# A cached-attention decode step with a gated MLP: the output weights in four transfers instead of five, six filler products instead of three, and two bias rows loaded by another engine

## The chip, the cores and the metric

The kernel runs on one core of a Trainium2 chip. Five engines share the work: TensorE (PE in the profile, its weight loads PEld) multiplies, VectorE (DVE) does the elementwise work and the reductions, ScalarE (ACT) copies and computes exponentials, GpSimd (POOL) only sets a few constants here, and SyncE (SP) issues transfers. Sixteen DMA engines bring data from the chip's memory. An engine works through its instructions in order and waits on semaphores. The metric is the device time of one execution in microseconds (us).

## The reference: what is computed

Two tokens (B = 2, one position each, D = 512) pass a layer normalisation; the result feeds two branches:

```python
xn = _layernorm(x)
s = attention(xn @ wq, k_cache, v_cache) @ wo     # 32 heads of 128, 8192 cached positions
h = gelu(_layernorm(xn) @ w1 + b1)                # 512 -> 1376
g = silu(h @ w2 + b2)                             # 1376 -> 512
out = x + s * g
```

Everything is float32. The caches hold 2 x 32 x 8192 x 128 numbers each, 268 MB for the keys and as much for the values. wq and wo have 8.4 MB each, w1 and w2 2.8 MB each; b1 has 5.4 KB and b2 2 KB.

## The kernel before

**The stream.** Nearly all transfers go through one queue, SyncE's, written out by hand in program order: w1, w2, wq, the first keys in two halves, then keys and values by turns, each turn (n = 0 to 31) 8.4 MB of keys and 8.4 MB of values, and at the end wo. A transfer is issued when its buffer has been read out, so SyncE waits for engines, not for data. There are two big buffers for keys and one (`vb`) for values. At the start `vb` holds all the small things of the boot stage instead, w1, w2, b1, b2 and the MLP's intermediates; the first values wait until the boot is through with it.

**The boot.** While the first weights arrive, the kernel makes its constants, normalises x, runs the whole MLP down to `gate` (function `mlp`), and forms the queries with wq. In `mlp`, each of three stretches of w1 ends with a product that adds b1 (L412); the four products that add b2 come last (L462). x, b1 and b2 are issued by ScalarE's queue (L337, L339), the rest by SyncE's (function `load`, L314).

**The turns.** VectorE multiplies keys by queries (L524) and sums (L531); TensorE, VectorE and ScalarE turn the sums into exponentials; TensorE multiplies them into the values (`weighted`, L575) and folds the result (L584). The turns 1 to 30 are a loop; the last one is written out behind it, and takes its values from a key buffer, so that `vb` is free for wo one turn earlier.

**The tail.** wo is read as 32 rows of 512 numbers per partition, and arrives in pieces; `WO_PIECES` gives the rows at which they begin and end. SyncE issues all pieces together once L575 of the turn before the last has read `vb` out. TensorE's order behind the last turn's products is: the sums of all heads (L632, L634), then `busy(3)`, then rows 0 to 23 of wo, then the rest. `busy(n)` (L562) issues n products of the identity with the queries, 128x512 each, into a scratch bank that nobody reads. Rows 0 to 23 (`WIDE` is 24) are multiplied as 128x512 products into `wide` (L648), which ScalarE then copies to SBUF (L651); rows 24 to 28 go as four 128x128 products each into `acc` (L657), then four products fold the copy of `wide` in (L662), then rows 29 to 31 follow (L657 again). Each row's product waits for its piece (function `piece`). VectorE multiplies `acc` by `gate` and adds x (L666, L667), and SyncE stores the result (L668).

Each float32 product stands in the trace as two matmul records, so that 24 products of L648 make 48 records.

Of the kernel before, what the change touches and what calls it, by code (L numbers as in the profile page):

```python
# [21 lines left out]
class Plan:  # L22
# [18 lines left out]
    def op(self, eng, fn, r=(), w=(), over=(), it=None, loop=False, dma=None):  # L41


        o = Op()
        o.eng, o.fn, o.it, o.loop, o.dma, o.tell = eng, fn, it, loop, dma, False
        need = {}

        def after(d, war):
            if d.dma is None and dma is None and d.eng == eng and (eng == "pe" or war):
                return  # L50
            if d.dma is None:
                if need.get(d.eng) is None or need[d.eng].idx < d.idx:
                    need[d.eng] = d
            else:
                k = ("dma", d.dma)
                if need.get(k) is None or need[k].idx < d.idx:
                    need[k] = d

        for k in r:
            if k in self.writer:  # L60
                after(self.writer[k], False)
        for k in list(w) + list(over):
            if k in self.writer:
                after(self.writer[k], False)
            for d in self.readers.get(k, ()):
                after(d, True)
        clock = self.clock[eng]
        need = {k: d for k, d in need.items() if clock.get(k, 0) < d.idx}
        o.deps = [(k, d) for k, d in need.items()
                  if not any(e is not d and e.done.get(k, 0) >= d.idx for e in need.values())]  # L70
        for _, d in o.deps:
            for k, v in d.done.items():
                clock[k] = max(clock.get(k, 0), v)
        own = eng if dma is None else ("dma", dma)
        self.count[own] = o.idx = self.count.get(own, 0) + 1
        o.done = dict(clock)
        o.done[own] = o.idx
        for k in w:
            self.writer[k] = o
            self.readers[k] = []  # L80
        for k in r:
            if k not in w:
                self.readers.setdefault(k, []).append(o)
        self.ops.append(o)
# [80 lines left out]
def decode_kernel(nc, x, kc, vc, wq, wo, w1, b1, w2, b2, out):  # L165
# [31 lines left out]
    op = plan.op  # L197

    def pe(fn, r=(), w=(), it=None, loop=False):
        op("pe", fn, r, w, it=it, loop=loop)  # L200

    def dve(fn, r=(), w=(), it=None, loop=False):
        op("dve", fn, r, w, it=it, loop=loop)
# [58 lines left out]
    def take(name, p, n, base=0, at=None):  # L262

        if at is None:
            at = used[0]
            used[0] += n
            assert used[0] <= KP * DH
        boot.append(name)
        return vb[base:base + p, at:at + n]
# [7 lines left out]
    b1_sb = take("b1", 1, F, R, at)  # L277
    b2_sb = take("b2", 1, D, R, at + F)
# [34 lines left out]
    def load(dst, src, sem, w, over=()):  # L313
        op("sp", lambda: nc.sync.dma_start(dst, src), (), w, over=over, dma=sem)  # L314

    def load_k(n):
        i = (n + 1) % 2
        if n in (0, N - 1):
            for s in range(2):
                load(kbuf[i][:, s * M:(s + 1) * M], kf[n][:, s * M:(s + 1) * M], f"k{i}{s}", [("kb", i, s)])  # L320
            return
        load(kbuf[i], kf[n], f"kb{i}", [("kb", i, s) for s in range(2)])


    WO_PIECES = (0, 16, 24, 29, 31, 32)
    WIDE, FOLD = WO_PIECES[-4:-2]


    load(w1_sb, w1.rearrange("(p c) f -> p c f", p=P), "w1", ["w1"])
    load(w2_sb, w2.rearrange("f n -> (f n)").rearrange("(p e) -> p e", p=P), "w2", ["w2"])  # L330
    load(wq_sb, wq.rearrange("(p c) n -> p c n", p=P), "wq", [("kb", 0, s) for s in range(2)])
    load_k(0)

# [1 line left out]
    dve(lambda: nc.vector.memset(eps_t, EPS), w=["eps"])  # L335
    act(lambda: nc.scalar.activation(warm, eps_t, AF.Sqrt), ["eps"], ["warm"])
    op("act", lambda: nc.scalar.dma_start(x_sb, x.rearrange("b s d -> (b s) d")), w=["x"], dma="x")  # L337
    for t, src, k in ((b1_sb, b1, "b1"), (b2_sb, b2, "b2")):
        op("act", lambda t=t, src=src: nc.scalar.dma_start(  # L339
            t.rearrange("o (k e) -> o k e", k=16), src.rearrange("(o k e) -> o k e", o=1, k=16)), w=[k], dma=k)  # L340


    pool(lambda: nc.gpsimd.memset(ident, 0.0), w=["ident"])
# [144 lines left out]
    for k in range(N // NB):  # L488

        b, e = divmod(k, HH // NB)  # L490
# [68 lines left out]
    def busy(n):  # L559

        for _ in range(n):
            pe(lambda: matmul(scratch[3], ident, Q[:, :512], start=True, stop=True),  # L562
               ["ident"] + [("Q", k) for k in range(512 // (NB * DH))], ["s3"])
# [55 lines left out]
    wo_r = wo.rearrange("(p c) n -> p c n", p=P)  # L619
    for i, (a, e) in enumerate(zip(WO_PIECES, WO_PIECES[1:])):  # L620
        load(wo_sb[:, a:e], wo_r[:, a:e], f"wo{i}", [("wo", i)], over=["vb"])
# [8 lines left out]
    for b in range(B):  # L630
# [2 lines left out]
           ["ones"] + [("ZR", n) for n in own], ["OA"])  # L633
        pe(lambda b=b: matmul(OA[:, b, :OC], Z[:, b * P:(b + 1) * P], mod, start=True, stop=True),  # L634
           ["mod"] + [("Z", n) for n in own], ["OA"])
    busy(3)
    dve(lambda: nc.vector.reciprocal(rl, OA[:, :, OC]), ["OA"], ["rl"])
    dve(lambda: nc.vector.tensor_tensor(out=on[:, ::RB], in0=OA[:, :, :OC],
                                        in1=rl.unsqueeze(2).to_broadcast([P, B, OC]), op=ALU.mult),
# [2 lines left out]
    def piece(c):  # L642
        return ("wo", max(i for i, a in enumerate(WO_PIECES[:-1]) if a <= c))

# [52 lines left out]
```

## Time and profile before

| | |
|---|---|
| median of 3 runs | 1300.4 us (1300.06 to 1300.45) |
| profiled execution: its own time | 1300.03 us |
| profiled execution: its span in the trace | 1298.2 us |
| DMA engines: share of the span in SyncE's queue | 99.7% |
| moved | 559.39 MB, 431 GB/s |
| VectorE busy | 1134.6 us, 87% |
| TensorE busy | 404.8 us, 31% |
| wo's five pieces, issue to landing | 19.0, 23.5, 26.1, 26.9, 27.1 us |

The span runs from the first to the last instruction of the traced execution; 1.83 us of its own time lie outside. The DMA engines are full from the first microseconds to the landing of wo's last piece, so the span is the length of the stream plus what lies before its first byte and behind its last. A line of a view of instructions gives its start, its length, the engine, the source line, the operation and the tiles, and in brackets how long the engine had been idle before it and what ended that.

### The profile page before, as it was taken

How to read it: one execution, taken by the hardware profiler on the slowest of the kernel's cores; microseconds unless marked ns; L12 is line 12 of the kernel's file. 1: busy time of each engine (PE TensorE's matmuls, PEld its weight loads, DVE VectorE, ACT ScalarE, POOL GpSimd, SP SyncE). 2: the span in 40 equal slices, each digit the busy share in tenths (PEclk: the TensorE clock that was granted, in tenths of full speed). 3: DMA queues.
4: the chain of work that ended last, by engine and by line, in shares of the span. 5: the costliest groups of instructions: out<-in, count | busy, mean ns of one | idle time of the engine just before them, and what ended most of it. 6: DMA issues, size and time to landing. Idle time of an engine off the chain costs nothing.

```text
span 1298.2 us, 6788 instructions
## 1 busy us (share of the span) xinstructions
PE 404.8 (31%) x2728; PEld 123.9 (10%) x2728; DVE 1134.6 (87%) x276; ACT 77.6 (6%) x250; POOL 1.4 (0%) x8
## 2 busy tenths in 40 slices
PE   5602333312333312333321333321233321233337
PEld 1100011000101000101000101100001000001103
DVE  3599999888889988889988888988888988888991
ACT  1100000000000000000000000000000000000000
POOL 0000000000000000000000000000000000000000
PEclk9856666556666656666656666656666655666658
DMA  9999999999999999999999999999999999999998
GB/s 406 445 423 440 430 432 436 426 444 428 438 430 432 438 426 440 430 434 434 428 442 428 438 430 430 440 426 440 430 434 434 430 438 430 438 430 430 427 433 363
DMA packets 10826, 559.39 MB, mean 431 GB/s; under 512 B 1208, under 2 KB 1216, under 8 KB 1476
## 3 DMA queue, kind: packets, MB, share of 16 engines
q1 hardware_dynamic: 10812, 559.29, 99.7%
q8 instruction: 4, 0.07, 0.0%
q14 instruction: 2, 0.02, 0.0%
q10 hardware_dynamic: 8, 0.01, 0.0%
HBM read 559.30 MB, written 0.00 MB: 431 GB/s over the span
## 4 chain that ended last, share of the span: by engine, by line
DMA 74%; PE 24%; DVE 1%; issue 0%; ACT 0%; SPq 0%; DVEq 0%
DMA vb<-in_A_v_cache_dram 72%; PE po L575 22%; DMA vb<-in_A_wo_dram 2%; PE s L410 1%; PE po L482 1%; PE s L452 0%; PE s L412 0%; PE acc L657 0%; DVE vb L418 0%; ACT L431 0%; DVE vb L356 0%; PE s L459 0%; SPq L314 0%; DVE vb L367 0%; DVE vb L444 0%
## 5 line engine op out<-in xcount | busy, mean ns | idle before, releaser
L524 DVE TENSOR_TENSOR kb<-kb,Q 128x8192 f32<-128x8192 f32 x64 | 555.5, 8681 | 105.2 <-DMA kb<-in_A_k_cache_dram 95.9
L531 DVE TENSOR_REDUCE sc<-kb 128x64 f32<-128x8192 f32 x64 | 552.3, 8665 | 0.0
L575 PE MATMUL po<-vb,PZ 128*8 128x512 f32 x1984 | 280.7, 730 | 292.8 <-DMA vb<-in_A_v_cache_dram 292.8
L547 PE MATMUL s<-nm,srow 1*128 1x2 f32 x64 | 18.7, 359 | 364.0 <-DVE nm L541 364.0
L575 PEld LDWEIGHTS po<-vb,PZ 128*8 128x8 f32 x1984 | 56.4, 103 | 491.0 <-issue 489.5
L538 PE MATMUL s<-ident,mx 128*1 128x128 f32 x32 | 11.8, 369 | 192.7 <-DVE mx L535 192.7
L547 PEld LDWEIGHTS s<-nm,srow 1*128 1x128 f32 x64 | 15.9, 307 | 373.3 <-DVE nm L541 373.3
L582 ACT COPY o<-po 128x512 f32<-128x512 f32 x32 | 18.7, 585 | 533.3 <-PE po L575 533.3
L548 ACT COPY bias<-s 128x2 f32<-128x2 f32 x32 | 5.1, 160 | 622.1 <-PE s L547 622.1
L584 PE MATMUL s<-mod,o 128*128 128x2 f32 x256 | 33.6, 253 | 22.1 <-ACT o L582 22.1
L584 PEld LDWEIGHTS s<-mod,o 128*128 128x128 f32 x256 | 31.0, 191 | 51.3 <-ACT o L582 51.3
L552 ACT ACTIVATE PZ<-sc,bias 64x128 f32<-64x128 f32 x64 | 25.5, 399 | 1.8
L538 PEld LDWEIGHTS s<-ident,mx 128*1 128x1 f32 x32 | 2.5, 79 | 196.2 <-DVE mx L535 165.7
L590 DVE TENSOR_TENSOR Z<-blk,s 128x8 f32 (+1 forms) x32 | 5.2, 163 | 13.3 <-PE s L584 13.3
L418 DVE COPY vb<-vb 2x384 f32<-2x384 f32 x4 | 1.8, 500 | 15.9 <-ACT vb L414 15.9
L410 PE MATMUL s<-vb 128*2 128x512 f32 (+1 forms) x24 | 12.5, 673 | 0.3 <-ACT vb L375 0.3
L552 ACT ACTIVATION_READ_ACCUMULATOR PZ<-sc,bias 64x1 f32 x64 | 11.8, 185 | 0.0
L666 DVE TENSOR_TENSOR gate<-acc,gate 128x128 f32<-128x128 f32 x1 | 0.3, 291 | 12.1 <-PE acc L657 12.1
L535 DVE TENSOR_REDUCE mx<-sc 128x1 f32<-128x128 f32 x32 | 9.2, 286 | 1.1
L556 ACT ACTIVATE ZR<-half,rs 128x8 f32 (+1 forms) x32 | 9.6, 301 | 4.1
L575 PE MATMUL po<-kb,PZ 128*8 128x512 f32 x64 | 9.4, 755 | 1.4 <-ACT PZ L552 1.4
L541 DVE TENSOR_REDUCE nm<-s 1x2 f32<-1x128 f32 x32 | 8.7, 272 | 0.3 <-PE s L538 0.3
(88 smaller groups left out, 84.5 us busy)
## 6 DMA issues: line engine op xcount, KB each, us to landing
kb<-in_A_k_cache_dram SPq DMA_DIRECT2D x4, 4096.0 KB, 43.5
kb<-in_A_v_cache_dram SPq DMA_DIRECT2D x2, 4096.0 KB, 40.9
vb<-in_B_w_dram SPq DMA_DIRECT2D x2, 2752.0 KB, 12.5
vb<-in_A_wo_dram SPq DMA_DIRECT2D x1, 4096.0 KB, 19.0
vb<-in_A_wo_dram SPq DMA_DIRECT2D x1, 2048.0 KB, 23.5
vb<-in_A_wo_dram SPq DMA_DIRECT2D x1, 1280.0 KB, 26.1
vb<-in_A_wo_dram SPq DMA_DIRECT2D x1, 512.0 KB, 26.9
vb<-in_A_v_cache_dram SPq DMA_DIRECT2D x31, 29.5
```

Of the source, the lines that this page charges most:

```text
L410: pe(lambda f=f, w=w, ph=ph, c=c: matmul(ph[:B, :w], yT[:, c, :], w1_sb[:, c, f:f + w], start=(c == 0), stop=False), ["yT", "w1"], [k])
L482: pe(lambda i=i, c=c, wv=wv, a=a, j=j, hd=hd: matmul(PO[R * j:R * j + NQ * B, :].rearrange("m (h d) -> m h d", d=DH), xnT[:, c, a:a + NQ * ...
L524: vector(n, n, lambda n: nc.vector.tensor_tensor(out=k, in0=k, in1=cols(Q, n * DH, DH).unsqueeze(1).to_broadcast([P, M, DH]), op=ALU.mult) ...
L531: vector(n, n, lambda n: nc.vector.tensor_reduce(out=SC[:, s * M:(s + 1) * M], in_=k, axis=AX.X, op=ALU.add), [("kb", i, s)], [("sc", s)])
L535: vector(n, n, lambda n: nc.vector.tensor_reduce(out=MX, in_=SC, axis=AX.X, op=ALU.max), [("sc", 0), ("sc", 1)], ["mx"])
L538: pe(lambda i: transpose(PM[:1, :P], MX, ident), ["mx", "ident"], ["s1"], it=n, loop=n > 0)
L547: pe(lambda i: matmul(PN[:, :U], srow, NM, start=True, stop=True), ["srow", "nm"], ["s2"], **one)
L552: act(lambda i, r=r, s=s: nc.scalar.activation(PZ[r, :, s, :], sc[r], AF.Exp, bias=BIAS[r, s:s + 1], scale=SCALE, accum_out=RS[r]), ["bias ...
L556: act(lambda i: nc.scalar.activation(cols(ZR, i * UP - UP, UP), half, AF.Copy, scale=RS), ["half"] + [("rs", s) for s in range(U)], [("ZR" ...
L575: pe(lambda i, t=t, j=j, v=v: matmul(PO[R * j:R * j + U * JW, :], PZ[:, t].rearrange("p s j -> p (s j)"), v[:, t * JW:(t + 1) * JW, :].rea ...
L582: act(lambda i: nc.scalar.copy(O4, PO), ["po"], ["o4"], **one)
L584: pe(lambda i, k=k: matmul(PT[:, :U], O4[:, k * DH:(k + 1) * DH], mod[:, k:U * JW:JW], start=(k == 0), stop=(k == JW - 1)), ["o4", "mod"], ...
```

## The change

- `WO_PIECES` becomes (0, 24, 29, 31, 32): wo arrives in four transfers, the first of which holds rows 0 to 23. `WIDE` and `FOLD` stay 24 and 29, and the products are the same in the same order.
- `busy(3)` becomes `busy(6)`.
- b1 and b2 are issued by SyncE, between w2 and wq, instead of by ScalarE behind x.

```diff
-    WO_PIECES = (0, 16, 24, 29, 31, 32)
+    WO_PIECES = (0, 24, 29, 31, 32)
     WIDE, FOLD = WO_PIECES[-4:-2]
...
     load(w2_sb, w2.rearrange("f n -> (f n)").rearrange("(p e) -> p e", p=P), "w2", ["w2"])
+    for t, src, k in ((b1_sb, b1, "b1"), (b2_sb, b2, "b2")):
+        load(t.rearrange("o (k e) -> o k e", k=16), src.rearrange("(o k e) -> o k e", o=1, k=16), k, [k])
     load(wq_sb, wq.rearrange("(p c) n -> p c n", p=P), "wq", [("kb", 0, s) for s in range(2)])
...
     op("act", lambda: nc.scalar.dma_start(x_sb, x.rearrange("b s d -> (b s) d")), w=["x"], dma="x")
-    for t, src, k in ((b1_sb, b1, "b1"), (b2_sb, b2, "b2")):
-        op("act", lambda t=t, src=src: nc.scalar.dma_start(
-            t.rearrange("o (k e) -> o k e", k=16), src.rearrange("(o k e) -> o k e", o=1, k=16)), w=[k], dma=k)
...
-    busy(3)
+    busy(6)
     dve(lambda: nc.vector.reciprocal(rl, OA[:, :, OC]), ["OA"], ["rl"])
```

## The prediction

> **What bounds the kernel now.** I read the page first, for the shares: SyncE's queue fills the DMA engines for 99.7% of the span. Then the chain that ended last, in order of time, for the tail:
>
> ```profile
> 1266.71 0.43 SPq L314
> 1267.15 0.06 issue
> 1267.20 26.14 DMA vb<-in_A_wo_dram
> 1293.34 0.04 issue
> 1293.38 1.31 PE acc L657 x34
> 1294.70 0.22 PE acc L662 x7
> 1294.91 0.83 PE acc L657 x23
> 1295.75 0.02 issue
> 1295.77 0.30 DVE gate L666
> ```
>
> The columns are start, length, and what ran. The end hangs on transfers up to 1293.34; behind that only 2.4 us of products, 0.6 us of VectorE and the store remain. Then TensorE's timeline of that stretch:
>
> ```profile
> 1266.99 1.05 PE L584 MATMUL s<-mod,o 128*128 128x2 f32 x8 [0.71 <-ACT o L582]
> ...
> 1283.03 2.82 PE L562 MATMUL s<-Q,ident 128*128 128x512 f32 x6
> 1285.78 3.67 PE L648 MATMUL wide<-vb,on 128*17 128x512 f32 x32
> 1290.30 1.94 PE L648 MATMUL wide<-vb,on 128*17 128x512 f32 x16 [0.85 <-DMA vb<-in_A_wo_dram]
> 1293.38 1.31 PE L657 MATMUL acc<-vb,on 128*17 128x128 f32 x40 [1.15 <-DMA vb<-in_A_wo_dram]
> 1294.50 0.41 PE L662 MATMUL acc<-o,mod 128*17 128x128 f32 x8
> 1294.72 0.99 PE L657 MATMUL acc<-vb,on 128*17 128x128 f32 x24
> ```
>
> TensorE keeps up with wo: rows 0 to 15 (x32) are done at 1289.45, before rows 16 to 23 are there; these (x16) are done at 1292.24, before the third piece is there. Third, the issues of wo on the page, with the time to landing:
>
> ```profile
> vb<-in_A_wo_dram SPq DMA_DIRECT2D x1, 4096.0 KB, 19.0
> vb<-in_A_wo_dram SPq DMA_DIRECT2D x1, 2048.0 KB, 23.5
> vb<-in_A_wo_dram SPq DMA_DIRECT2D x1, 1280.0 KB, 26.1
> vb<-in_A_wo_dram SPq DMA_DIRECT2D x1, 512.0 KB, 26.9
> ```
>
> Added to the issues (1266.34, 1266.71, 1267.20) that makes landings at 1285.3, 1290.2 and 1293.3; the last two pieces follow at about 1294.6 and 1295.2 (26.9 and 27.1 us from issues some 0.4 us apart). Fourth, TensorE's granted clock, in stretches of time (columns: stretch, its length, busy time and instructions of PE, PEld, DVE, ACT, POOL, granted clock, DMA share, GB/s). I come back to these:
>
> ```profile
> 1187.09:1190.50 3.41, 2.25 (x20) 1.07 (x12) 3.41 (x1) 0.58 (x1) 0.00 (x0) 1.00 0.93 404
> 1190.50:1193.91 3.41, 0.00 (x0) 0.00 (x0) 3.41 (x1) 0.00 (x0) 0.00 (x0) 0.50 1.11 480
> 180.16:183.57 3.41, 2.60 (x24) 1.17 (x16) 3.41 (x2) 0.58 (x1) 0.00 (x0) 1.00 1.11 480
> 183.57:186.98 3.41, 0.00 (x0) 0.00 (x0) 3.41 (x1) 0.00 (x0) 0.00 (x0) 1.00 0.84 365
> 1289.49:1292.90 3.41, 1.94 (x16) 0.47 (x16) 0.00 (x0) 0.58 (x1) 0.00 (x0) 1.00 0.96 398
> ```
>
> **The change part by part. Landing of the first piece.** Its 24 rows are the bytes of the first two pieces of before, behind the same stream, so it lands when the second did, 1290.2. What a transfer costs beside its bytes bounds the gain of one fewer: rows 16 to 23 took 4.9 us (1285.3 to 1290.2), 0.61 a row; the last two pieces, two rows and one row, took about 1.9 us between 1293.3 and 1295.2, 0.63 a row. Two per cent of a row is 0.02 us; the roundings allow 0.3. On the other side a whole issue on SyncE (0.43 us) could be saved, were the queue short; it is not, since the issue is 19 us ahead of its landing. I take 0, between a gain of 0.4 and a loss of 0.
>
> **TensorE behind it.** Before, rows 0 to 15 ran from 1285.78, beside the transfer of the next piece. That cover is gone: nothing of wo can start before 1290.25, and all 24 rows stand behind the wait, with the rest of wo queued behind them on TensorE. Sixteen rows took 3.67 us and eight took 1.94: 1.73 for eight more (0.216 a row), and 0.21 of run-out. So 24 rows from 1290.29 take 24 x 0.216 = 5.18 us until the next product can begin: 1295.47. Rows 24 to 31 and the fold took from 1293.38 to the end of the last record at 1294.72 + 0.99 = 1295.71, 2.33 us, in which TensorE waited some 0.15 us for the last piece; that wait goes, since all pieces have landed by 1295.2. So acc ends at 1295.47 + 2.18 = 1297.65, that is **1.9 us later**. ScalarE's copy of `wide` could come in between: it starts at 1295.47 + 0.21 + 0.06 = 1295.74 and takes the 0.58 us of L651, to 1296.32; the fold that needs it stands behind 40 records of L657, which take 1294.50 - 1293.38 = 1.12 us, to 1296.59. It is hidden, by 0.27 us. From the end of acc on nothing changes (L666, L667, the store).
>
> The price depends on TensorE's clock. At full clock it is the above. At half clock throughout, the same products take double (the records of L575 go by fours in 0.85 us at clock 0.50 and in 0.43 at 1.00): 5.2 us more. These are the ends; I take full clock, for the reason below, and price a part of half clock as a rival.
>
> **Three more products.** Six records of L562 took 2.82 us, so three products more take 6 x 0.43 = 2.6 us, to 1288.4 instead of 1285.85. TensorE waits for the piece until 1290.25 anyway, so they cost nothing; 1.85 us of wait are left as cover. Were the piece there before 1288.4, each further us would be theirs. They write a scratch bank that nobody reads; `on` (L638), which L648 also needs, is done at 1283.7 and waits for no product of L562.
>
> **b1 and b2 on SyncE.** ScalarE loses two issues (0.53 us together, from 1.47 on); its next work, the copy L384 at 6.14, waits for TensorE, so nothing is gained. SyncE gets two issues more, at 0.27 to 0.43 us each, in front of wq, the two halves of the first keys and all later ones. It issues w1 at 0.74 and wq at 1.65, while w1 and w2 keep the DMA engines busy until about 16.7 (12.5 us from issue to landing, mean of the two, 6.5 us apart): delay of wq's issue 0.5 to 0.9 us, under 14 us of cover. The bytes are the same. New is that b1 and b2 stand behind w2. b1 is needed by L412 at 17.02, b2 by L462 at 39.0. A small transfer's time is not shown by the page; between nothing and 1.4 us behind w2 (about what a packet of the first transfers took), b1 lands between 16.7 and 18.1, so L412, and the whole boot behind it on TensorE, may wait 0 to 1.1 us. What waits for the boot: the first values and the second keys, issued at 46.45 to 46.82. The queue then still holds the rest of wq and both halves of the first keys, which land 43.5 us after their issues, the second after 55; the stream doesn't run dry if the boot is 1.1 us late. VectorE starts on the keys 1.1 us later (48.90 now), and issues the third keys at 83.41, when the values in flight land only at 95.09, 11.7 us of cover. I take 0.
>
> **Sum.** 0 + 1.9 + 0 + 0: span 1300.1, own time of the profiled execution 1300.03 + 1.9 = 1301.9. That execution lies 0.37 below the median of the runs, so the median becomes **1302.3**, 0.15% more. 0.2% (2.6 us) is about what a measurement of this kernel can tell from no change; my forecast lies inside, the threshold is at 1303.0.
>
> **Does the clock hold over the wait?** The granted clock changes at 1262.18, 1269.02 and 1275.84 (from the one-us slices that hold these points: 0.91, 0.51, 0.58), and earlier at 1231.46: always a multiple of 3.41 us apart. So it is decided window by window on a fixed grid. The rows above are windows on that grid. The one from 1187.09 has 2.25 us of products, of which 1.05 are L584's tiny ones (128x2), so 1.2 of large ones: half clock follows. The one from 180.16 has 1.55 of large ones, that from 1289.49 has 1.94: full clock follows. The limit lies between 1.2 and 1.55 us of large products. After the change TensorE idles from 1288.4 to 1290.3. On the grid of this profile the two windows concerned hold 2.3 (1286.08 to 1288.4) and 2.6 us (1290.3 to 1292.9): full clock holds. But the grid need not stand so in another execution. If its lines lie d earlier, TensorE also reaches full clock d earlier than 1275.84, and the filler ends d/2 earlier. For d = 1.2 the window from 1288.29 holds 1291.70 - 1290.3 = 1.4 us, on the limit; for d = 2.2, the most (a line earlier still finds too little of L575, which begins at 1271.0), it holds 0.4. Lines later than here make it no worse. So about 0.85 to 1.2 of 3.41, 25 to 35% of positions, lose the clock.
>
> [...]
>
> **Rivals.**
> - *Half clock behind the wait (slower).* With the grid as above, clock 0.50 begins at 1290.7 to 1291.8 and lasts one full window, since that one is filled with L648 (the row of a filled window, from 1272.4, is followed by full clock). 3.41 us at half clock lose 1.7 us: 1.9 + 1.7 = 3.6, median 1304.0 (1303.5 to 1304.5). For it: the row at 1187.09; against: this profile's own grid. It decides when a window on the grid holds under some 1.4 us of large products.
> - *The first piece lands sooner* because one transfer in place of two is cheaper. Each us earlier takes one off, down to 1288.4, where the filler ends: then acc ends at 1288.4 + 5.18 + 2.18 = 1295.8, no change, 1300.4. The landings per row above speak against it. [...]
> - *b1 late starves the stream (slower).* It would have to delay the boot by over 9 us, to the landing of the first keys; the price is the excess. By the rows it is at most 1.1 us late.
>
> **How the numbers follow.** Full clock 0.56, of which 0.50 within 0.2% and 0.06 above (if the transition to acc or the copy costs 0.7 us more); own range 1301.8 to 1303.1. Half clock 0.32, above. Earlier landing 0.05: 0.04 within, 0.01 faster. b1 late 0.03, above. Unnamed 0.04, halved between the ends. Faster 0.03, same 0.54, slower 0.43. The range reaches down to an early landing of half a us and some noise (1301.4) and up to the half-clock case with its upper bound (1304.5), leaving out about 0.15.
>
> **What would show it.** In the new profile: a single group L648 of 48 records starting at 1290.2 to 1290.4 after the end of L562 near 1288.4, with about 1.9 us idle before it; L657 directly behind without a wait for wo; acc ending 1.9 us later (3.6 with clock 0.50 in a slice after 1290.7); L412 at most 1.1 us late; DMA share unchanged. Wrong it would be if L648 starts well before 1290, if L657 waits for ScalarE's copy, or if a slice before 1290 shows a gap in the DMA.

## The result, and the profile after

The changed kernel takes 1301.72 us in the median of 22 runs (1301.46 to 1303.33), the kernel before, run beside it, 1300.13 (1300.03 to 1300.45). Between the medians lie 1.6 us, or 0.12%. The ratio of the means is 1.0016, with a 95% interval of 1.0010 to 1.0022: 2.1 us. Both are inside the 0.2% that the forecast named. The runs do not scatter about the median. They lie in two groups with nothing between them: 13 runs from 1301.46 to 1301.84, and 9 from 1303.07 to 1303.33. The profiled execution belongs to the slower group (1303.33, span 1302.0).

TensorE's timeline of the changed kernel, for the same stretch as before (columns as before; the lines of the file are one lower, L561 was L562, L647 was L648, L656 was L657):

```profile
1282.12 5.40 PE L561 MATMUL s<-Q,ident 128*128 128x512 f32 x12
1290.44 7.07 PE L647 MATMUL wide<-vb,on 128*17 128x512 f32 x48 [2.93 <-DMA vb<-in_A_wo_dram]
1297.32 1.29 PE L656 MATMUL acc<-vb,on 128*17 128x128 f32 x40
1298.41 0.41 PE L661 MATMUL acc<-o,mod 128*17 128x128 f32 x8
1298.63 0.85 PE L656 MATMUL acc<-vb,on 128*17 128x128 f32 x24
```

The two groups of L648 have become one of 48 records. It begins 2.93 us after the filler has ended, when the first piece lands, and everything behind it follows without a wait: the transfers no longer set the end, TensorE does. The chain that ended last says the same. Before, it stayed with the transfers up to 1293.34; now it leaves them at 1290.40:

```profile
1265.37 25.02 DMA vb<-in_A_wo_dram
1290.40 0.04 issue
1290.44 7.07 PE wide L647 x48
1297.51 1.09 PE acc L656 x40
1298.60 0.22 PE acc L661 x8
1298.82 0.69 PE acc L656 x24
```

The 7.07 us hold the second matter. Stretches of 3.41 us with their granted clock (third number from the end; the first pair after the length is TensorE's busy time):

```profile
1283.93:1287.34 3.41, 3.41 (x9) 1.32 (x7) 0.00 (x0) 0.00 (x0) 0.00 (x0) 1.00 1.07 461
1287.34:1290.75 3.41, 0.48 (x5) 0.19 (x8) 0.00 (x0) 0.00 (x0) 0.00 (x0) 1.00 0.76 323
1290.76:1294.17 3.41, 3.41 (x20) 0.87 (x16) 0.00 (x0) 0.00 (x0) 0.00 (x0) 0.50 0.80 323
1294.17:1297.58 3.41, 3.41 (x44) 1.31 (x40) 0.00 (x0) 0.01 (x1) 0.00 (x0) 1.00 0.03 13
```

In this execution the idle time fell wholly into one window, which held 0.48 us of products; the next window ran at clock 0.50, was filled, and full clock came back. The two bias rows are on the queue where they were put; the first product that needs b1 waits for it by a quarter of a us:

```profile
16.27 1.01 PE L411 MATMUL s<-vb,ones 1*2 1x512 f32 x2 [0.24 <-DMA vb<-in_B_b_dram]
```

### The profile page after: what moved, and what is told of

It reads as the page before. It is cut to its first block, busy times and chain, and to the rows that moved or that the text cites. A ratio compares the mean times of both kernels' runs of the same rounds, so it can differ in the third digit from the quotient of the medians.

```text
span 1302.0 us, 6799 instructions
## 1 busy us (share of the span) xinstructions
PE 406.8 (31%) x2734; PEld 125.2 (10%) x2734; DVE 1134.7 (87%) x276; ACT 77.6 (6%) x250; POOL 1.4 (0%) x8
## 4 chain that ended last, share of the span: by engine, by line
DMA 75%; PE 24%; issue 0%; DVE 0%; ACT 0%; SPq 0%
DMA vb<-in_A_v_cache_dram 72%; PE po L574 22%; DMA vb<-in_A_wo_dram 2%; DMA vb<-in_B_b_dram 1%; PE wide L647 1%; PE po L481 1%; PE s L409 0%; PE s L451 0%; PE s L411 0%; PE acc L656 0%; DVE vb L417 0%; ACT L430 0%; PE s L458 0%; SPq L314 0%; PE s L423 0%
## 5 line engine op out<-in xcount | busy, mean ns | idle before, releaser
L574 PE MATMUL po<-vb,PZ 128*8 128x512 f32 x1984 | 281.7, 732 | 296.8 <-DMA vb<-in_A_v_cache_dram 296.8
L574 PEld LDWEIGHTS po<-vb,PZ 128*8 128x8 f32 x1984 | 56.5, 103 | 495.9 <-issue 495.9
L583 PE MATMUL s<-mod,o 128*128 128x2 f32 x256 | 33.6, 253 | 22.1 <-ACT o L581 22.1
L583 PEld LDWEIGHTS s<-mod,o 128*128 128x128 f32 x256 | 31.0, 191 | 51.3 <-ACT o L581 51.3
L574 PE MATMUL po<-kb,PZ 128*8 128x512 f32 x64 | 8.5, 682 | 1.4 <-ACT PZ L551 1.4
```

The lines of the kernel that those rows point to most:

```text
L574: pe(lambda i, t=t, j=j, v=v: matmul(PO[R * j:R * j + U * JW, :], PZ[:, t].rearrange("p s j -> p (s j)"), v[:, t * JW:(t + 1) * JW, :].rea ...
L583: pe(lambda i, k=k: matmul(PT[:, :U], O4[:, k * DH:(k + 1) * DH], mod[:, k:U * JW:JW], start=(k == 0), stop=(k == JW - 1)), ["o4", "mod"], ...
```

## The experiments

My theory had three parts: rows 0 to 15 of wo lost the cover that they had under the next piece's transfer, which makes the span 1.9 us longer; a window with too little work costs a further 1.7 us of half clock in some executions; the filler and the bias rows cost nothing. One thing was left to explain: in the quick group the span had grown by 2.0 us (1300.2 against 1298.2), but the time by only 1.5. The rest of the time, outside the first and the last instruction, had shrunk.

Spans and the time outside are given for the same executions throughout, and all medians of before are between 1300.13 and 1300.20.

**Five pieces again, the rest of the change kept.**

```diff
-    WO_PIECES = (0, 24, 29, 31, 32)
+    WO_PIECES = (0, 16, 24, 29, 31, 32)
```

> The changed kernel with wo in five pieces again (rows 0 to 15 in the first), six filler products and b1, b2 on SyncE kept. Theory (the loss is the cover taken from rows 0 to 15): the first piece lands at 1285.4, the filler ends at about 1288.4, so the 24 rows start there and end at 1288.2 + 5.18 = 1293.4, as the third piece lands (1293.3). The end comes back to that of before: span 1298.2 to 1298.4, no second group of runs, and L648's line shows no wait for wo of over 0.3 us. Rival (the filler or the bias rows cost time themselves): the span stays above 1299.

Measured: 1299.75 us (1299.51 to 1299.99, 11 runs), spans 1298.2 to 1298.7, one group. Its timeline:

```profile
1282.77 5.40 PE L561 MATMUL s<-Q,ident 128*128 128x512 f32 x12
1288.10 5.38 PE L647 MATMUL wide<-vb,on 128*17 128x512 f32 x48
1293.58 1.32 PE L656 MATMUL acc<-vb,on 128*17 128x128 f32 x40
```

The 24 rows follow the filler with no wait at all and end as the third piece lands. The whole of the longer span, and the second group, come from the first transfer's size. The six filler products, though they now push rows 0 to 15 back by over 2 us, cost nothing: what they push back had slack.

**Only the bias rows moved.** This is the kernel before with nothing but b1 and b2 taken to SyncE:

```diff
+    for t, src, k in ((b1_sb, b1, "b1"), (b2_sb, b2, "b2")):
+        load(t.rearrange("o (k e) -> o k e", k=16), src.rearrange("(o k e) -> o k e", o=1, k=16), k, [k])
     load(wq_sb, ...)
...
-    for t, src, k in ((b1_sb, b1, "b1"), (b2_sb, b2, "b2")):
-        op("act", lambda t=t, src=src: nc.scalar.dma_start(...), w=[k], dma=k)
```

> The kernel before with b1 and b2 issued by SyncE, nothing else. In the changed kernel the span grew by 2.0 us in the quick group, but the time by only 1.5: the time outside the span fell from 1.83 to 1.33 us. Theory (two issues fewer on ScalarE's queue shorten what lies outside the span): span 1298.2, time 1299.7, 0.4 to 0.5 us under before. Rival (the four pieces do that, or the profile of before is off by that much): time 1300.1, outside 1.8. In both the first product with b1 waits at most 1.1 us.

Measured: 1299.67 us (1299.34 to 1299.94, 11 runs), against 1300.04 to 1300.47 for the kernel before beside it (29 runs). The spans are the same (1298.0 to 1298.6 against 1298.2 to 1298.7); outside the span lie 1.28 to 1.45 us against 1.77 to 1.96. So the move is worth half a us, none of it where the profile shows instructions. The ratio is 0.9996 with an interval of 0.9987 to 1.0005, which does not exclude no change, but no run of one kernel reaches into the runs of the other.

**Eight filler products, and three.** Two sizes of `busy` in the changed kernel:

```diff
-    busy(6)
+    busy(8)        # the other kernel: busy(3)
```

> The changed kernel with eight filler products instead of six. Theory (the slow group is the granted clock, lost in a window of 3.41 us that holds under some 1.4 us of large products): eight products end at 1289.0 to 1290.4, the idle time before the first piece is at most 1.3 us, every window holds over 2 us, so no run falls in the slow group: all within 1301.4 to 1302.0. Rival (the slow group comes from something else, the DMA or the rest of the chip): about 4 in 10 runs are at 1303.1 to 1303.4 as with six products.

> The changed kernel with three filler products as before. Theory (clock): TensorE idles from about 1285.9 to 1290.4, over 3.41 us, so the clock is lost in every execution, and comes back only after a filled window: 2.6 to 6 us of the products run at half clock, 1.3 to 3.0 us lost. No run in the quick group: all between 1302.8 and 1304.6. Rival (an idle stretch of any such length costs nothing, the two groups come from elsewhere): 6 in 10 runs at 1301.5 to 1301.8.

Measured with eight: 1301.58 us, all 11 runs within 1301.47 to 1301.70. With three: 1303.68, 7 runs spread from 1302.97 to 1304.53. The slow group is gone in the one and has swallowed all runs in the other. The lines of L647 with eight, then the windows of the kernel with three:

```profile
1290.43 5.38 PE L647 MATMUL wide<-vb,on 128*17 128x512 f32 x48 [0.29 <-DMA vb<-in_A_wo_dram]
1295.62 1.28 PE L656 MATMUL acc<-vb,on 128*17 128x128 f32 x40
...
1296.93 0.85 PE L656 MATMUL acc<-vb,on 128*17 128x128 f32 x24
```

```profile
1284.33:1287.74 3.41, 0.65 (x2) 0.00 (x0) 0.00 (x0) 0.00 (x0) 0.00 (x0) 1.00 1.03 447
1287.74:1291.15 3.41, 0.73 (x4) 0.19 (x8) 0.00 (x0) 0.00 (x0) 0.00 (x0) 0.50 0.83 350
1291.15:1294.56 3.41, 3.41 (x20) 0.78 (x16) 0.00 (x0) 0.00 (x0) 0.00 (x0) 0.50 0.76 305
1294.57:1297.98 3.41, 3.41 (x48) 1.33 (x43) 0.00 (x0) 0.10 (x1) 0.00 (x0) 1.00 0.01 4
```

With eight products the 24 rows take 5.38 us, against 7.07 in the profile of the changed kernel: the half clock cost 1.69 us. With three, the window from 1284.33 holds 0.65 us and loses the clock, the next one holds 0.73 and does not bring it back, and only the filled one from 1291.15 does: 4.15 us of the products (1290.42 to 1294.57) run at half clock. The wait itself is not what costs: with eight products TensorE is hardly ever idle, and still the span is 1300.3, 2 us above that of five pieces. Here filler kept the clock and did not give back the cover.

**How large the first piece may be.** Twenty rows, and 22, in a first piece of five:

```diff
-    WO_PIECES = (0, 24, 29, 31, 32)
+    WO_PIECES = (0, 20, 24, 29, 31, 32)        # the other kernel: (0, 22, 24, 29, 31, 32)
```

> The changed kernel with wo in pieces of 20, 4, 5, 2 and 1 rows, six filler products. Theory (the loss is what the products of the first piece lack of cover): 20 rows land at about 1287.9, before the filler ends at 1288.2, so the 24 rows end at 1293.4, when the third piece lands: span as with five pieces and 16 rows first (1298.3), time 1299.7, one group. Rival (each row that is moved into the first piece costs its share, 1.5 us for 8 rows): 0.75 us more than with 16 rows, 1300.5.

> The changed kernel with wo in pieces of 22, 2, 5, 2 and 1 rows, six filler products. Theory: 22 rows land at 1289.1 to 1289.2, the 24 rows end 5.18 us later, at 1294.3, 0.8 us behind the third piece: span 0.6 to 0.9 above that of five pieces with 16 rows first (1298.9 to 1299.2), time 1300.3 to 1300.6; idle before the first row 0.9 us at most, so no second group. Rival (share per row): 1.1 us more, 1300.8.

Measured with 20 rows: 1299.64 us (10 runs), as with 16. With 22: 1300.33 (10 runs), spans 1298.9 to 1299.1, 0.7 us more. The lines of L647, and of L656 behind it, with 20 rows first, where no wait is left, and then with 22:

```profile
1288.50 5.37 PE L647 MATMUL wide<-vb,on 128*17 128x512 f32 x48
1293.68 1.28 PE L656 MATMUL acc<-vb,on 128*17 128x128 f32 x40
...
1289.23 5.38 PE L647 MATMUL wide<-vb,on 128*17 128x512 f32 x48 [0.58 <-DMA vb<-in_A_wo_dram]
1294.42 1.28 PE L656 MATMUL acc<-vb,on 128*17 128x128 f32 x40
```

The loss is no share per row. It is nothing up to a corner and then the whole delay of the landing: the first piece lands, 5.19 us later L656 can begin, and only what lies past the third piece's landing (1293.3 to 1293.5) counts. With 22 rows that is about 0.9 us, with 24 it is 2.2, less the wait for the last pieces that goes.

**The bias rows back on ScalarE, the rest of the change kept.** The reverse of the second experiment: the kernel before with four pieces and six products, and nothing else.

```diff
-    WO_PIECES = (0, 16, 24, 29, 31, 32)
+    WO_PIECES = (0, 24, 29, 31, 32)
...
-    busy(3)
+    busy(6)
```

> The changed kernel with b1 and b2 issued by ScalarE's queue as before; four pieces and six filler products kept. Theory (0.5 us outside the span hang on these two issues): span 1300.2 in the quick group and 1301.9 in the slow one, outside the span 1.8, times 1302.0 to 1302.2 and 1303.6 to 1303.8. Rival (the pieces or the filler shorten what lies outside as well): times 1301.6 and 1303.2.

Measured: seven runs from 1301.77 to 1302.00 and three from 1303.48 to 1303.68. The spans are those of the changed kernel (1300.0 to 1300.2 and 1301.8 to 1302.0); outside lie 1.67 to 1.85 us, median 1.72, against 1.30 to 1.49 there. That is 0.35 of the half us, so most of what the time outside lost goes with the bias rows; the missing 0.1 us (1.72 against the 1.85 or so of the kernel before) went with the pieces or the filler. I had expected 1.8, and times of 1302.0 to 1302.2.

**x moved as well.** The kernel of the second experiment with x, too, issued by SyncE, between w1 and w2:

```diff
     load(w1_sb, ...)
+    load(x_sb, x.rearrange("b s d -> (b s) d"), "x", ["x"])
...
-    op("act", lambda: nc.scalar.dma_start(x_sb, ...), w=["x"], dma="x")
```

> The kernel before with b1, b2 and x all issued by SyncE: x between w1 and w2, b1 and b2 between w2 and wq; five pieces, three filler products. x then lands behind w1, at about 10 us, and the boot ends some 5 us later, under the 9 us that the queue holds. Theory (each issue of ScalarE saves outside the span): span 1298.3, outside about 1.1, time 1299.4. Rival (the saving is a single step, made already by b1 and b2): outside 1.35, time 1299.7. Should the boot not be covered after all, the span grows above 1298.6.

Measured: 1299.73 us (1299.50 to 1300.14, 10 runs), outside 1.29 to 1.44. No further gain: the saving is a step that the move of b1 and b2 had already made. The run also shows that the boot may slip by 3.6 us. x comes 4.2 us later (the first product of the boot at 9.70 instead of 5.46), the second keys are issued at 50.01 instead of 46.45, and the span stays at 1298.3.

## Why the prediction was right, and where it was off

- *Landing of the first piece*, taken as that of the second before, 1290.2: it landed at 1290.40 (25.02 us from 1265.37). One transfer fewer brought nothing forward, and the rival of an earlier landing falls. In the seven profiles in which a product waits for row 23, it begins between 1290.30 (before) and 1290.45, whatever the pieces and the queue of the bias rows: at 1290.44 with four pieces and the bias rows on ScalarE, at 1290.45 with only the bias rows moved. So the 0.15 us more than in the profile of before can be put down to neither alone. The forecast's 0.61 a row was that of the 8 rows of the second piece, its 0.63 that of rows 29 to 31 together. From the landings of before (1293.34, 1294.60, 1295.23) rows 29 and 30 and row 31 take 0.63 us a row each.
- *24 rows in 5.18 us, rows 24 to 31 in 2.18 us, at full clock*: with eight products L647 begins at 1290.43, L656 at 1295.62 (5.19 us), and the last record ends at 1296.93 + 0.85 = 1297.78 (2.16 us). The span of the quick group is 1300.1 to 1300.5, for a forecast of 1300.1.
- *ScalarE's copy hidden by 0.27 us*: L661 follows L656 without a wait in every profile; in the changed kernel's the copy ends at 1298.16 and L661 begins at 1298.41.
- *Three more filler products at nothing*: shown by five pieces with six products. With four pieces they are a gain: three products take 1303.68 us there, six 1301.72.
- *b1 0 to 1.1 us late, under 9 us of cover*: L411 waits 0.24 us here, not at all in the profile with only the bias rows moved, and the span doesn't show it; moving x made the boot 3.6 us late, and that was still covered. The landing behind w2, between 16.7 and 18.1, was wrong: b1 is there by 16.27, and w2 lands at 16.73. The 1.4 us of that range is the longest packet of the first transfers in the trace of before; in the median they took 0.82.
- *Half clock 25 to 35% of executions, 1.7 us*: 9 of 22 here and 3 of 10 with the bias rows on ScalarE, 12 of 32 together, which is 38% and too few to tell from 35, at 1.69 us. The windows that decide are on the grid of 3.41 us as told: the granted clock of the changed kernel's profile changes at 1270.28, 1273.69, 1290.75 and 1294.17, one, five and one times 3.41 us apart. In the profile they begin 2.15 us earlier than before (1287.34 against 1289.49); for 2.2 the forecast had 0.4 us of work in the window, and it held 0.48. Eight and three products move the share to none and all. One step was wrong: the forecast used this share of the executions as the chance that the median is slow (0.32). Both groups occur side by side in one series, so a share below half leaves the median in the quick group.
- *The sum*: here the prediction was off. "ScalarE loses two issues [...] so nothing is gained" failed. I looked for a gain inside the span, found that the copy L384 waits for TensorE, and carried the 1.83 us outside the span over unchanged. They became 1.37, and the moved bias rows account for most of that (0.5 us alone, 0.35 undone). So the quick group came 1.5 us above before instead of 1.9, and the slow one 3.1 instead of 3.6; the medians of the two groups are 1301.61 and 1303.24 where I had 1302.3 and 1304.0. Of these 0.7 to 0.8 us some 0.3 are that the kernel before came out at 1300.13 over more runs, not at 1300.4; nearly all of the rest is the time outside.

In the two profiles with four pieces and six products the idle stretches are 2.93 and 2.98 us, less than a window of 3.41, and in the first the window that half clock followed was not idle: it held 0.48 us of work.

The changed kernel is thus slower by its first part alone; its second part limits that loss, and its third is a small gain. The kernel before with the bias rows moved (1299.67 us) lies below both, by 0.5 and by 2.0 us; a first piece of 20 rows does as well (1299.64).

## What to carry to other kernels

Where a stream sets the end, the consumer of the last transfer should have nothing left of the earlier ones: a larger piece costs nothing until the work that waits for it, laid end to end from its landing, reaches past the landing that it used to be hidden under (here nothing with 20 rows, 0.7 us with 22), and from there on the whole delay. Filler in such a wait kept the clock here and did nothing else: with eight products the three windows from 1285.88 on held 3.12 us of work or more, and no run fell into the second group; with six, one held 0.48 us in the profile and half clock followed. A median can hide that some executions are in a second group, which a list of the runs shows at once. And when small issues are moved between queues, compare the time outside the span too.

## What the runs showed of the hardware that was not expected

Moving two small issues (b1 and b2) from ScalarE's queue to SyncE's shortened the time by about 0.5 us without a trace inside the span: outside it lie 1.77 to 1.96 us before (29 runs), and 1.28 to 1.45 with nothing but these two moved (11 runs). Moving a third issue added nothing (1.29 to 1.44). What happens there is not shown by the profile, and stays open: no run tells the two issues fewer on ScalarE from the two more on SyncE, or moves only one. With wo in four pieces the bias rows bring back only 0.35 us of it, while with the bias rows on SyncE four pieces and five leave the same outside (medians 1.37 and 1.35), so the two don't simply add up.

The way back to full clock had a limit as well. In the turns of the two profiles, before and after, windows of the grid at full clock that held up to 1.24 us of the values' products (L574; after, from 1225.90, with 1.05 us of the tiny ones of L583 beside them) were followed by half clock, and those that held 1.54 or more (before, from 180.16, again with 1.05 us of the tiny ones) by full clock; none lies between. At half clock, windows with up to 2.56 us of these products (after, from 946.01) were followed by half clock again, and those with 2.61 or more (after, from 829.96) by full clock. These products take twice as long at half clock (four records 0.85 us against 0.43); by that, as an estimate, 2.56 and 2.61 us are the work of 1.28 and 1.30 us at full clock, between the 1.24 and the 1.54.

A small transfer was there before a large one that had been issued ahead of it in the same queue: in the changed kernel's profile b1, 5.4 KB, issued at 1.65, by 16.27, and w2, 2752 KB, issued at 1.19, at 16.73.
